# A banded attention with a gated mixture layer on one core: a new hand-over order of all engines' steps, with new bank and engine choices and re-measured costs in its planner

## The chip, the cores and the metric

The kernel runs on one core of one Trainium2 chip. The time is the device time of one execution in microseconds (us). Before the change three executions took 366.51, 365.14 and 366.31 us, so the median is 366.31 us. Nothing runs on the other cores.

## The reference

For 8 batches and 8 heads there are 512 local and 32 global positions of 64 numbers each. Local queries see the global keys and the local keys at most 32 positions away; global queries see every key. The 8 heads of a position together make a row of 512 numbers, and the 576 rows of a batch go through a gated layer: a causal convolution of five taps per channel makes the gate.

```python
k_all = np.concatenate([k_g, k_l], axis=2)
v_all = np.concatenate([v_g, v_l], axis=2)
s_g = scale * np.matmul(q_g, k_all.transpose(0, 1, 3, 2))
out_g = np.matmul(sm(s_g), v_all)
mask = np.abs(pos[:, None] - pos[None, :]) <= window
s_ll = np.where(mask, s_ll, -1000000000.0)
s_l = np.concatenate([s_lg, s_ll], axis=-1)
a_l = sm(s_l)
out_l = np.matmul(a_l, np.concatenate([v_g, v_l], axis=2))
...
gate = 1.0 / (1.0 + np.exp(-gate_pre))
val = x @ w_val
return (gate * val @ w_out).astype(np.float32)
```

## The kernel before, in words

The work is cut into 32 units (a pair of heads of one batch, numbered u), four to a batch b. Every step of a unit or a batch is a named task, and the string `ORDER` lists all 1,425 of them; each engine executes its own tasks strictly in that order, so the list is the schedule. A name can carry the engine after a colon (`xc13:DVE`) and, after an @, the PSUM bank or banks (there are 8) that the task's product is written to.

The tasks, with the lines of the profile:

- `iq`, `iv`, `wi` issue the loads of a unit's q and k (624 KB), of its v (975 KB) and of a weight (512 KB) on SP's queue (L405). The function `transfer` ties each such load to the last TensorE instruction that stands ahead of it in the list: SP waits for that one, so a load's place in the list is a time on TensorE.
- `s` are a unit's local scores (L552: 32 small products, a tiling of 64 rows by 32 columns of the array), `gs` a batch's global scores (L482, the same tiling). `mx` adds the mask and takes the row maxima on VectorE (L564), `exp` runs on ScalarE (L571), `t` transposes the result (L577), `tc` copies it out of PSUM, `av` multiplies by v (L588, a tiling of 128 by 32). `gmax`, `gexp`, `gt`, `gtc` and `gav` (L520) do the same for the global queries.
- `norm` divides (L598), `xt` transposes (L604), `xc` copies out. `xh` and `xl` split x in a high and a low half, `tap` and `conv` are the convolution (L640), `sig` the sigmoid. For the first two units the convolution runs as `pc` on TensorE (L665).
- `g1.b.e.t` are three 128x128x512 products each with w_val (L689), 16 such tasks a batch; `gv` multiplies by the gate, `gh` and `gl` split the result again, `g2.b.r.e` are three such products with w_out (L711), `ob` copies out, `st` stores. The group called g does the global rows at the end.
- `w0` to `w7` with `.s0` to `.s7` and `.high` turn a weight's 64-bit floats into two halves, on VectorE and ScalarE.

On TensorE there are therefore groups of many short instructions (an `s` is 64 weight loads and 64 multiplies by the profile's count) between long wide products (a `g1` part is three and three). TensorE's instructions come from memory over a DMA queue of their own (q8 in the profile).

The class `Plan` holds the tasks. Its method `order` walks `ORDER`, works out when each task would start by costs and lags written as numbers, and checks the bank of each; the list itself was found outside by annealing against those costs. At run time the numbers have one effect only: where the plan sees a gap on TensorE near the start, `keep_clock` puts in idle 128x512 products (L775) that fill it. In `order`, TensorE's instructions are counted in units (`FETCH`), and every 256 instructions a new packet of them has to be there; `BLOCK`, `STALL` and `AHEAD` say that it is asked for 72 instructions ahead of the packet's bound and needed 192 behind it, and `IDLE`, `BEGINS`, `LANDS`, `BUSY` how long it takes beside a load. `SWITCH` is the price of a change of tiling on TensorE between the classes of `MODE`.

Of the kernel before, what the change touches and what calls it, by code (L numbers as in the profile page):

```python
# [19 lines left out]
KW = 5  # L20
# [42 lines left out]
xc4 sig0 iq9 norm5 gv.0.0 w7.s0:ACT sig1 w7.s1 w6.s0:ACT w6.s1 s7@27 iq10 gv.0.1 sig2 g1.0.2.0@4 sig3 g1.0.2.1 g1.0.2.2
gt1.1@0 mx7.0 mx7.1 g1.0.2.3 g1.0.3.0@5 w7.s2 gtc1.1 gh.0.0 exp7.1 gl.0.0 gav1.1 exp7.0 w6.s2 gh.0.1 g1.0.3.1 av6@2
xt5@7 t7.1@0 tc7.1 w7.s3 w6.s3 w7.s4 w6.s4 g1.0.3.2 t7.0@1 g1.0.3.3 iv9 norm6 w6.s5 xh4 w7.s5 w6.s6 tc7.0 gv.0.2
g2.0.0.0@0 w6.high av7@2 xt6@4 w6.s7 gl.0.1 xc5 w7.high iq11 gh.0.2 w7.s6 gv.0.3 g2.0.0.1 gl.0.2 iv10 s8@71 w7.s7 gh.0.3
gl.0.3 norm7 g2.0.0.2 g2.0.0.3 g2.0.1.0@5 g2.0.1.1 g2.0.1.2 s9@23 mx8.0 ob.0.0 gnorm1 iv8 mx8.1 xl4 mx9.0 exp8.0 st.0.0
gs2@06 exp8.1 gx1@2 mx9.1 g2.0.1.3 gxc1 xh5 tap5 g2.0.2.0@3 ob.0.1 gmax2.0 t8.1@2 halo4:ACT t8.0@5 iq12 g2.0.2.1
tap4:ACT tc8.1 st.0.1 gexp2.0 conv4.0 g2.0.2.2 conv4.1 iv11 halo5:ACT xt7@2 tc8.0 conv4.2 gmax2.1 g2.0.2.3 xl5 iq13
av8@0 exp9.1 t9.1@5 ob.0.2 gexp2.1 norm8 g2.0.3.0@3 conv5.0 g2.0.3.1 gt2.0@0 exp9.0 conv4.3 conv5.1 st.0.2 xc7 xh7  # L70
conv5.2 tap7 tc9.1 g2.0.3.2 s10@67 t9.0@2 xl7 conv5.3 tc9.0 gtc2.0 g2.0.3.3 xt8@5 mx10.0 mx10.1 halo7:ACT exp10.0 xc6
iq14 g1.1.0.0@2 av9@0 conv7.0 xh6 gav2.0@7 s11@46 ob.0.3 norm9 conv7.1 g1.1.0.1 gt2.1@0 xl6 t10.0@3 mx11.0 mx11.1
conv7.2 halo6:ACT exp10.1 tap6:ACT t10.1@4 g1.1.0.2 conv6.0 gtc2.1 g1.1.0.3 tc10.1 xt9@4 conv7.3 conv6.1 exp11.1
g1.1.1.0@6 gav2.1 conv6.2 tc10.0 xc8:DVE av10@0 conv6.3 iq15 g1.1.1.1 norm10 iv12 g1.1.1.2 g1.1.1.3 sig4 sig5 xc9
tap9:ACT iv14 gv.1.0 g1.1.2.0@0 tap8 g1.1.2.1 gh.1.0:DVE g1.1.2.2 gnorm2 iv13 xh8 gv.1.1 g1.1.2.3 gx2@1 s12@67 gs3@42
gl.1.0 sig6 gh.1.1:DVE sig7 gv.1.2 gl.1.1 gh.1.2 xl8 g1.1.3.0@0 gmax3.0 g1.1.3.1 gxc2 exp11.0 mx12.0 mx12.1 g1.1.3.2
t11.1@1 g1.1.3.3 gmax3.1 gl.1.2 gv.1.3 halo9:ACT t11.0@7 gexp3.0 exp12.0 g2.1.0.0@6 tc11.1 tc11.0 halo8 gt3.0@4
gh.1.3:DVE gtc3.0 conv8.0 conv8.1 iq16 xt10@0 t12.0@7 exp12.1 gl.1.3 xh9 conv8.2 g2.1.0.1 conv8.3 xl9 xc10 g2.1.0.2
gexp3.1 av11@4 st.0.3 tc12.0 t12.1@1 g2.1.0.3 norm11 halo10:ACT xh10:DVE iv15 conv9.0 conv9.1 ob.1.0 tc12.1 g2.1.1.0@0
xl10 g2.1.1.1 s13@74 av12@2 mx13.0 xt11@1 g2.1.1.2 conv9.2 mx13.1 tap10 g2.1.1.3 g2.1.2.0@4 exp13.0 conv9.3 t13.0@5  # L80
g2.1.2.1 exp13.1 xc11 iq17 t13.1@1 conv10.0 norm12 conv10.1 xh11 s14@76 g2.1.2.2 g2.1.2.3 mx14.0 tc13.1 conv10.2 exp14.0
tc13.0 mx14.1 ob.1.2 st.1.0 conv10.3 xt12@1 xc12 av13@2 gav3.0@4 tap11 s15@56 norm13 halo11:ACT t14.0@1 exp14.1 xl11
mx15.0 xh12 iq18 t14.1@7 conv11.0 conv11.1 tc14.1 st.1.2 gt3.1@2 g2.1.3.0@5 gtc3.1 g2.1.3.1 iq19 gav3.1 ob.1.1:DVE xl12
tc14.0 av14@0 xt13@7 gnorm3 gx3@4 exp15.0 g2.1.3.2 iv16 g2.1.3.3 mx15.1 exp15.1 st.1.1 gxc3:DVE g1.2.0.0@4 conv11.2
conv11.3 norm14 xc13:DVE t15.0@6 sig8 t15.1@2 g1.2.0.1 iv17 tc15.1:DVE sig9 s16@70 iv18 mx16.0 mx16.1 xh13 g1.2.0.2
ob.1.3:DVE tap12:ACT halo12 g1.2.0.3 conv12.0 gv.2.0 conv12.1 tc15.0 xt14@7 conv12.2 g1.2.1.0@6 sig10 conv12.3 sig11
g1.2.1.1 g1.2.1.2 exp16.1 xc14 g1.2.1.3 av15@4 gh.2.0 tap14:ACT gv.2.1 norm15 gs4@02 iv19 halo14 gl.2.0 s17@76 iq20
mx17.0 halo13 t16.1@4 gmax4.0 exp17.0 gmax4.1 xl13 gh.2.1 gexp4.0 g1.2.2.0@5 g1.2.2.1 tc16.1 xt15@7 g1.2.2.2 g1.2.2.3
gl.2.1 gexp4.1 g1.2.3.0@0 g1.2.3.1 exp16.0 gv.2.2 xh14:DVE mx17.1 tap13 gt4.0@4 t16.0@1 g1.2.3.2 t17.0@6 g1.2.3.3 gtc4.0
tc17.0 gav4.0@4 conv13.0 exp17.1 gt4.1@2 xl14 conv13.1 gtc4.1 gh.2.2 gv.2.3 tc16.0 gh.2.3 st.1.3 g2.2.0.0@6 t17.1@5  # L90
conv13.2 conv14.0 conv13.3 g2.2.0.1 gav4.1 tc17.1:DVE xc15 iq21 av17@0 av16@2 gl.2.3 gnorm4 xh15 gl.2.2 halo15:ACT
g2.2.0.2 norm16 iv21 g2.2.0.3 xt16@7 g2.2.1.0@2 tap15 g2.2.1.1 g2.2.1.2 g2.2.1.3 ob.2.0 g2.2.2.0@6 s18@34 xl15 conv15.0
norm17 s19@50 ob.2.1 conv14.1 st.2.1 g2.2.2.1 xt17@2 conv14.2 mx18.0 mx18.1 iv20 g2.2.2.2 mx19.0 mx19.1 conv14.3
g2.2.2.3 g2.2.3.0@3 st.2.0 exp18.1 g2.2.3.1 t18.1@0 exp19.0 gx4@1 exp19.1 iq22 conv15.1 g2.2.3.2 g2.2.3.3 xc17 conv15.2
xh17:DVE t19.1@2 gxc4 tc19.1:DVE g1.3.0.0@1 exp18.0 conv15.3 t18.0@5 g1.3.0.1 t19.0@2 g1.3.0.2 xl17 tap17 halo17 xc16
g1.3.0.3 conv17.0 ob.2.3 tc18.0 iq23 tc19.0:DVE tc18.1 av18@4 conv17.1 ob.2.2 sig12 norm18 av19@6 conv17.2 g1.3.1.0@0
sig13 tap16 xt18@4 g1.3.1.1 gv.3.0 g1.3.1.2 sig14 norm19 xh16 halo16 gh.3.0 g1.3.1.3 iv22 s20@15 gs5@62 conv17.3 gv.3.1
xc18 mx20.0 mx20.1 exp20.1 iv23 tap18 xl16 s21@40 g1.3.2.0@5 gl.3.0 gh.3.1 g1.3.2.1 gmax5.0 g1.3.2.2 st.2.2 mx21.0
exp20.0 halo18 t20.1@1 mx21.1 g1.3.2.3 t20.0@4 conv16.0 gv.3.2 gexp5.0 gh.3.2:DVE gl.3.1 sig15 gmax5.1 xt19@6 tc20.0
tc20.1 st.2.3 g1.3.3.0@7 conv16.1 iq24 gexp5.1 g1.3.3.1 conv16.2 g1.3.3.2 conv16.3 g1.3.3.3 gt5.0@0 g2.3.0.0@4 g2.3.0.1  # L100
av20@2 gtc5.0 xc19 gav5.0@5 xh18 s22@60 gv.3.3 gh.3.3:DVE gl.3.2 norm20 exp21.0 t21.0@7 xh19 exp21.1 g2.3.0.2 tap19:ACT
gl.3.3 g2.3.0.3 halo19:ACT xl19 xl18 mx22.0 g2.3.1.0@1 g2.3.1.1 tc21.0:DVE conv18.0 conv18.1 exp22.0 mx22.1 ob.3.0
gt5.1@2 g2.3.1.2 t21.1@4 iq25 tc21.1:DVE t22.0@7 gtc5.1 conv18.2 g2.3.1.3 xt20@0 gav5.1 conv18.3 av21@2 exp22.1 xc20
iq26 g2.3.2.0@4 conv19.0 gnorm5 t22.1@0 gx5@5 g2.3.2.1 ob.3.1 conv19.1 g2.3.2.2 xh20:DVE s23@16 conv19.2 tc22.1 st.3.1
# [895 lines left out]
```

## Time and profile before

| what | value |
|---|---|
| median of 3 executions | 366.31 us (365.14 to 366.51) |
| the profiled execution | 369.17 us, of which the span from first to last instruction is 367.4 us |
| busy, TensorE multiplies / weight loads | 353.4 us / 278.8 us |
| busy, VectorE / ScalarE | 322.7 us / 243.8 us |
| granted TensorE clock, mean | 0.995 |
| HBM read / written | 56.87 MB / 8.91 MB |

The span is the time between the first and the last instruction; the other 1.8 us of the profiled execution lie around it. PE is TensorE, PEld its weight loads, DVE VectorE, ACT ScalarE, SP the engine whose queue issues loads; a `q` behind a name is that engine's sequencer. In the timeline a row has its start, its length and the instruction with xcount; what stands in brackets is idle time just before it and what ended that. "issue" is idle time for which the profile shows nothing that was waited for. Multiplies overlap in the array, so a row's length is not the time it costs: the distance between two starts is.

### The profile page before, as it was taken

The numbers are of one execution on the slowest core, as the hardware profiler recorded it, in microseconds if no ns is written. First come the engines' busy times: TensorE is split into PE (matmuls) and PEld (weight loads), VectorE is DVE, ScalarE is ACT, GpSimd is POOL, SyncE is SP. The second block draws the span as 40 slices with busy tenths as digits, with TensorE's granted clock in tenths as the row PEclk, the third lists the DMA queues.
The fourth block names the chain that finished last, engine by engine and source line by source line (L and its number), as shares of the span: only waits on it lengthen the run. The fifth ranks groups of instructions, "written<-read, shape, count | busy, mean of one in ns | idle before, by whom it ended". The sixth has DMA issues, their size and how long they took to land.

```text
span 367.4 us, 14722 instructions
## 1 busy us (share of the span) xinstructions
PE 353.4 (96%) x6334; PEld 278.8 (76%) x6334; DVE 322.7 (88%) x1079; ACT 243.8 (66%) x566; POOL 0.8 (0%) x7
## 2 busy tenths in 40 slices
PE   7799999999999999999997999999999999999995
PEld 3556668778788788787886888788877888888894
DVE  4999999999999998998797899999889876997972
ACT  4898799867978689673787858777775456333030
POOL 0000000000000000000000000000000000000000
PEclk9999999999999999999998999999999999999999
DMA  8996896389276459816555155570775101010223
GB/s 291 396 347 200 281 378 249 108 318 307 79 228 248 152 157 320 309 60 215 180 191 168 63 196 184 190 269 4 243 244 221 61 2 59 30 58 2 86 86 86
DMA packets 17248, 66.72 MB, mean 182 GB/s; under 512 B 1952, under 2 KB 4000, under 8 KB 17184
## 3 DMA queue, kind: packets, MB, share of 16 engines
q1 hardware_dynamic: 12240, 57.12, 44.5%
q10 hardware_dynamic: 4944, 8.67, 6.5%
q8 instruction: 49, 0.80, 0.9%
q14 instruction: 15, 0.12, 0.1%
HBM read 56.87 MB, written 8.91 MB: 179 GB/s over the span
## 4 chain that ended last, share of the span: by engine, by line
PE 78%; DVE 12%; DMA 6%; issue 2%; ACT 1%; SPq 1%; DVEq 0%; ACTq 0%
PE psum L711 24%; PE psum L689 23%; PE psum L588 7%; PE psum L552 7%; PE psum L577 7%; PE psum L604 3%; DMA v<-in_vw_dram 3%; DVE pm L564 3%; PE psum L520 2%; DMA wraw<-in_w_out_dram 2%; DVE gate L640 1%; PE psum L500 1%; PE psum L482 1%; DMA qk<-in_qk_dram 1%; DVE xs L598 1%
## 5 line engine op out<-in xcount | busy, mean ns | idle before, releaser
L571 ACT ACTIVATE pm<-pm,mx 128x128 f32<-128x128 f32 x256 | 80.8, 393 | 22.7 <-DVE mx L564 22.4
L640 DVE SCALAR_TENSOR_TENSOR gate<-xc,cw,gate 128x512 f32<-128x512 f32 x120 | 87.7, 747 | 1.6 <-ACT gate L386 0.4
L564 DVE CUSTOM_DVE_ANT_0 pm<-psum,mask 128x128 f32<-128x128 f32 x256 | 57.3, 286 | 3.8 <-PE psum L552 3.7
L689 PE MATMUL psum<-xh,wvh 128*128 128x512 f32 x128 | 54.9, 429 | 0.1
L711 PE MATMUL psum<-woh,gh 128*128 128x512 f32 x128 | 54.7, 428 | 0.0
L689 PE MATMUL psum<-xl,wvh 128*128 128x512 f32 x128 | 51.0, 398 | 2.0 <-issue 2.0
L689 PE MATMUL psum<-xh,wvl 128*128 128x512 f32 x128 | 50.7, 396 | 0.0
L711 PE MATMUL psum<-woh,gl 128*128 128x512 f32 x128 | 50.4, 394 | 0.0
L711 PE MATMUL psum<-wol,gh 128*128 128x512 f32 x128 | 50.1, 391 | 0.0
L577 PE MATMUL psum<-ident,pm 128*128 128x128 f32 x256 | 39.8, 281 | 1.1 <-ACT pm L571 1.0
L552 PE MATMUL psum<-qk 64*32 64x128 f32 x2048 | 37.0, 273 | 2.3 <-issue 1.4
L577 PEld LDWEIGHTS psum<-ident,pm 128*128 128x128 f32 x256 | 30.8, 142 | 10.9 <-ACT pm L571 3.1
L588 PEld LDWEIGHTS psum<-v,pts 128*32 128x32 f32 x2048 | 30.5, 109 | 9.9 <-issue 4.1
L552 PEld LDWEIGHTS psum<-qk 64*32 64x32 f32 x2048 | 29.0, 105 | 11.2 <-issue 5.5
L588 PE MATMUL psum<-v,pts 128*32 128x65 f32 x2048 | 34.7, 221 | 1.5 <-DMA v<-in_vw_dram 1.3
L393 ACT COPY pts<-psum 128x512 f32<-128x512 f32 x50 | 28.3, 584 | 7.3 <-PE psum L577 7.1
L393 ACT COPY ob<-psum 128x512 f32<-128x512 f32 x27 | 15.7, 585 | 23.4 <-PE psum L711 20.2
L393 ACT COPY xc<-psum 128x512 f32<-128x512 f32 x27 | 15.7, 582 | 21.9 <-DVE gate L640 11.2
L697 DVE TENSOR_TENSOR gv<-psum,gate 128x512 f32<-128x512 f32 x32 | 21.9, 685 | 9.5 <-PE psum L689 9.3
L689 PEld LDWEIGHTS psum<-xh,wvh 128*128 128x128 f32 x128 | 24.4, 190 | 5.9 <-issue 1.3
L689 PEld LDWEIGHTS psum<-xl,wvh 128*128 128x128 f32 x128 | 24.3, 190 | 5.8 <-issue 2.5
L711 PEld LDWEIGHTS psum<-woh,gl 128*128 128x128 f32 x128 | 24.0, 188 | 5.7 <-DVE gl L703 0.4
(109 smaller groups left out, 559.7 us busy)
## 6 DMA issues: line engine op xcount, KB each, us to landing
v<-in_vw_dram SPq DMA_DIRECT2D x32, 975.0 KB, 7.2
qk<-in_qk_dram SPq DMA_DIRECT2D x32, 624.0 KB, 4.7
out_dram<-ob ACTq DMA_DIRECT2D x32, 256.0 KB, 2.2
wraw<-in_w_val_dram SPq DMA_DIRECT2D x4, 512.0 KB, 12.2
wraw<-in_w_out_dram SPq DMA_DIRECT2D x4, 512.0 KB, 4.7
mask<-in_mask_dram SPq DMA_DIRECT2D x1, 256.0 KB, 4.5
out_dram<-obg SPq DMA_DIRECT2D x4, 64.0 KB, 1.7
out_dram<-obg ACTq DMA_DIRECT2D x4, 64.0 KB, 2.0
```

The source lines that it names most:

```text
L393: A.copy(out, in_)
L520: on_pe(T.matmul(ag[SG * c:SG * c + SG, :], pgt[:k, s, SG * c:SG * c + SG], vt[:k, w, h, :], start=(n == 0), stop=(n == len(steps) - 1)))
L552: on_pe(T.matmul((sx, sy)[h][32 * j:32 * j + 32, i, :], qkt[rows, 32 * m:32 * m + 32], qkt[rows, k0:k0 + P], start=True, stop=True))
L564: V.tensor_tensor_reduce(out=pm[:, h, i, :], in0=s[:, i, :], in1=mask[:, i, :], op0=ALU.add, op1=ALU.min, scale=-SCALE, scalar=3.0e38, acc ...
L571: A.activation(out=pm[:, h, i, :], in_=pm[:, h, i, :], func=AF.Exp, bias=mx[:, c:c + 1], scale=-1.0)
L577: on_pe(T.transpose(pt[:, i, :], pm[:, h, i, :], ident))
L588: on_pe(T.matmul(ax[32 * j:32 * j + 32, h, E1 * i:E1 * i + E1], pts[:, h, i, 32 * j:32 * j + 32], vt[:, block_win(4 * i + j), h, :], start ...
L604: on_pe(T.transpose(xt[:, P * i:P * i + P], xs[:, i].rearrange("p h d -> p (h d)"), ident))
L640: V.scalar_tensor_tensor(out=acc, in0=xc[:, k:k + SL], scalar=cw[:, u % NDT, k:k + 1], in1=acc, op0=ALU.mult, op1=ALU.add)
L689: on_pe(T.matmul(box["pv", e], w[:, e, t * P:t * P + P], x, start=(t == 0 and q == 0), stop=(t == NDT - 1 and q == 2)))
L697: V.tensor_tensor(out=box["gv", e], in0=box["pv", e], in1=gates[x0 + e], op=ALU.mult)
L711: on_pe(T.matmul(box["po", r], g[:, e, rs], w[:, e, :], start=(e == 0 and q == 0), stop=(e == NDT - 1 and q == 2)))
```

## The change

`ORDER` is replaced as a whole: the same 1,425 tasks in another order, with other banks, and with another engine for 94 of them (VectorE's instructions go from 1,041 to 1,047 rows, ScalarE's table loads from 18 to 20). The planner's numbers are new, its model of an instruction fetch lets a fetch wait to the end of any load under way when it is sent, without a limit, and a fetch takes DMA time itself; transposes become a tiling class of their own.

```diff
-sig13 tap16 xt18@4 g1.3.1.1 gv.3.0 g1.3.1.2 sig14 norm19 xh16 halo16 gh.3.0 g1.3.1.3 iv22 s20@15 gs5@62 conv17.3 gv.3.1
-xc18 mx20.0 mx20.1 exp20.1 iv23 tap18 xl16 s21@40 g1.3.2.0@5 gl.3.0 gh.3.1 g1.3.2.1 gmax5.0 g1.3.2.2 st.2.2 mx21.0
+g1.3.1.2 sig15 xh18 g1.3.1.3 st.2.2 gv.3.1 av19@2 norm19 s20@51 mx20.0 s21@04 st.2.3 mx21.0 gs5@26 mx20.1 g1.3.2.0@5
+iv21 iv23 exp20.0 g1.3.2.1 exp21.0 g1.3.2.2 mx21.1 gmax5.0 iq24 g1.3.2.3 conv17.0 gmax5.1 g1.3.3.0@4 gh.3.1 gl.3.1
...
-IDLE, BEGINS, LANDS, BUSY = 3050, 1400, 1200, 2600
-MODE = {"s": 0, "gs": 0, "av": 1, "gav": 1}
-SWITCH = ((0, 185, 185), (130, 0, 110), (110, 90, 0))
+IDLE, BEGINS, LANDS, SPREAD, TAKES = 3050, 150, 800, 0, 900
+MODE = {"s": 0, "gs": 0, "av": 1, "gav": 1, "t": 2, "xt": 2, "gt": 2, "gx": 2}
+SWITCH = ((0, 190, 190, 295), (112, 0, 113, 192), (94, 93, 0, 0), (92, 93, 0, 0))
...
-                now = MODE.get(kind(t.name), 2)
+                now = MODE.get(kind(t.name), 3)
...
-                        wait = [b - sent for a, b in self.loads if a <= sent < b]
-                        here = sent + IDLE + min([BUSY, max(wait, default=0)])
+                        wait = [b - sent for a, b in self.loads if a - SPREAD <= sent < b + SPREAD]
+                        here = sent + IDLE + max(wait + [0])
+                        if free["DMA"] > sent:
+                            free["DMA"] += TAKES
...
-        plan.add(f"gs{b}", "PE", 1050, lambda b=b: g_s(b), [f"lq{u}" for u in units] + ([f"gs{b - 1}"] if b else []),
+        plan.add(f"gs{b}", "PE", 916, lambda b=b: g_s(b), [f"lq{u}" for u in units] + ([f"gs{b - 1}"] if b else []),
```

The other costs change in the same way (an `av` from 1040 to 933, a `g2` from 700 to 682, a `t` from 380 to 436, and so on); no instruction's own operands change.

On TensorE, around unit 16's scores (rows named qk, 32 short products) in batch 2 the list had, before, transposes, a wide product, the scores, and wide products again:

```order
L577 MATMUL psum<-ident,pm_2490 128x128 x8
L689 MATMUL psum<-xh_2135,wvh 128x512
L689 MATMUL psum<-xl_2136,wvh 128x512
L689 MATMUL psum<-xh_2135,wvl 128x512
L552 MATMUL psum<-qk_2120 32x128 x32
L689 MATMUL psum<-xh_2197,wvh 128x512
L689 MATMUL psum<-xl_2198,wvh 128x512
```

In the changed kernel, whose line numbers are 5 higher, there stand at unit 16's scores:

```order
L716 MATMUL psum<-woh,gl_1966 128x512
L593 MATMUL psum<-v_2153,pts_2317 32x65 x32
L593 MATMUL psum<-v_2249,pts_2470 32x65 x32
L557 MATMUL psum<-qk_2340 32x128 x32
L609 MATMUL psum<-ident,xs_2663 128x128 x4
L694 MATMUL psum<-xh_2027,wvh 128x512
L694 MATMUL psum<-xl_2028,wvh 128x512
```

The two products with v of units 14 and 15 now stand right ahead of the scores, and the transposes of unit 14 between the scores and the next wide product. Over the whole list, short groups (`s`, `gs`, `av`, `gav`) that a wide product (`g1`, `g2`, `pc`) follows directly go from 24 to 8, and short groups that follow a wide product or a transpose from 47 to 43.

On TensorE around unit 21's scores in batch 3, before, the end of the global scores of batch 5 (the last of 16 such rows), the scores and the products of task `g1.3.2.0`:

```order
L482 MATMUL psum<-qk_3313 32x160
L552 MATMUL psum<-qk_3009 32x128 x32
L689 MATMUL psum<-xh_2511,wvh 128x512
L689 MATMUL psum<-xl_2512,wvh 128x512
L689 MATMUL psum<-xh_2511,wvl 128x512
```

In the changed kernel the scores of units 20 and 21 stand together, behind the products with v of unit 19 and ahead of the global scores:

```order
L694 MATMUL psum<-xh_3100,wvl 128x512
L593 MATMUL psum<-v_2772,pts_3241 32x65 x32
L557 MATMUL psum<-qk_2921 32x128 x32
L557 MATMUL psum<-qk_3034 32x128 x32
L487 MATMUL psum<-qk_2921 32x384
L487 MATMUL psum<-qk_3034 32x384
```

The loads of v that the list had ahead of unit 20's and unit 21's scores (`iv22`, `iv23` in the diff) have moved: `iv22` far ahead, into batch 2, and `iv23` behind the whole of the short groups and one task of wide products.

More of the change, by code (lines that the diff above doesn't have):

```diff
@@ L71 @@
[L71 to L80, printed above, removed]
@@ new lines @@
+g2.0.2.0@4 conv4.0 g2.0.2.1 conv5.2 t9.0@5 conv4.1 st.0.0 iv11 tc8.1 conv4.2 exp9.1 tc9.0 g2.0.2.2 g2.0.2.3 gs2@26
+t9.1@5 ob.0.2 g2.0.3.0@4 st.0.1 iv10 conv4.3 conv5.3 gmax2.0 tc8.0 xt7@0 g2.0.3.1 xc6 g2.0.3.2 gmax2.1 xc7 g2.0.3.3
+av8@0 xh6 ob.0.3:DVE xl6 xh7 tc9.1 av9@4 iq12 iq13 halo7 gexp2.0 s10@23 st.0.3 halo6 gexp2.1 tap6:ACT norm8 xt8@0
+g1.1.0.0@1 xl7 mx10.0 gt2.0@6 tap7:ACT gtc2.0 norm9 conv7.0 g1.1.0.1 mx10.1 s11@67 conv7.1 exp10.0 exp10.1 gav2.0@4
+t10.0@5 conv6.0 mx11.0 iq14 conv6.1 conv7.2 iq15 exp11.0 tc10.0 g1.1.0.2 g1.1.0.3 mx11.1 gt2.1@2 conv6.2 conv7.3 gtc2.1
@@ L291, in put @@
                     self.rings[name][2][key] = t.end + LAG[t.eng]
-            if t.eng == "DMA":
-                self.loads = self.loads[-11:] + [(t.start + BEGINS, t.end + LANDS)]
+            if t.eng == "DMA" and t.name != "first":
+                self.loads = self.loads[-15:] + [(max([t.start + BEGINS] + [b for _, b in self.loads[-1:]]), t.end + LANDS)]
             line.append(t)
@@ L444, in weight @@
         wraws[k] = load
-        for n, ns in enumerate(((("DVE", 320), ("ACT", 520)), (("DVE", 320), ("DVE", 320)), 360, 560, 320, 540, 320, 540)):
+        for n, ns in enumerate(((("DVE", 338), ("ACT", 585)), (("DVE", 336), ("DVE", 336)), 336, 602, 336, 602, 336, 602)):
             plan.add(f"w{k}.s{n}", *((ns, 0) if n < 2 else ("DVE", ns)), lambda n=n: step(n),
@@ L853, in attention_moe @@
+        plan.add(f"xh{u}", (("ACT", 515), ("DVE", 335)), 0, lambda u=u: l_xh(u), [f"xc{u}"], take=[("xh", u), ("xl", u)], lock=True)
         plan.add(f"xl{u}", (("DVE", 600), ("DVE", 600)), 0, lambda u=u: l_xl(u), [f"xh{u}"], lock=True)
@@ L872, in attention_moe @@
         plan.add(f"fv{u}", "FREE", 0, lambda: None, [f"av{u}", f"gav{b}.0", f"gav{b}.1"], give=[("v", u)])
-    plan.add("cw", "DVE", 1300, taps, ["craw"], take=[("mx", "cv")], give=[("mx", "cv")])
+    plan.add("cw", "DVE", 1410, taps, ["craw"], take=[("mx", "cv")], give=[("mx", "cv")])
     plan.given("start", 0.0)
```

248 lines of the change are left out of this document (128 added, 120 removed).

## The prediction

> **What bounds the kernel now.** I read the page first, then TensorE's timeline, then windows and SP's queue.
>
> ```profile
> PE 353.4 (96%) x6334; PEld 278.8 (76%) x6334; DVE 322.7 (88%) x1079; ACT 243.8 (66%) x566; POOL 0.8 (0%) x7
> ...
> q8 instruction: 49, 0.80, 0.9%
> ...
> PE 78%; DVE 12%; DMA 6%; issue 2%; ACT 1%; SPq 1%; DVEq 0%; ACTq 0%
> ```
>
> TensorE is busy in 96% of the span and holds 78% of the chain that ended last. The change alters none of its products, so the time can only come from four things: the start, changes of tiling, waits, and the end. The start first, a row of TensorE's timeline:
>
> ```profile
> 14.27 1.11 PE L588 MATMUL psum<-v,pts 128*32 128x65 f32 x64 [1.34 <-DMA v<-in_vw_dram]
> ```
>
> and the windows from 5 to 80 us (length, then busy time by engine; the row "sum" adds all four):
>
> ```profile
> 5.00:20.00 15.00, 12.29 (x317) 7.64 (x316) 13.57 (x73) 11.54 (x35) 0.00 (x0) 1.00 1.05 400
> 60.00:80.00 20.00, 19.75 (x396) 15.12 (x396) 19.62 (x79) 15.17 (x35) 0.00 (x0) 1.00 0.60 214
> sum 75.00, PE 70.15 PEld 49.34 DVE 71.69 ACT 62.02 POOL 0.00; mean PE 17.54 PEld 12.33 DVE 17.92 ACT 15.50 POOL 0.00
> ```
>
> The first product with v waits for its load until 14.27 us, and from 5 to 80 us VectorE is busy 71.69 of 75 us: it, not TensorE, sets when the first `g2` can run. Behind 80 us TensorE waits seldom, and where it does the releaser is "issue". These are the largest such places:
>
> ```profile
> 93.49 0.29 PE L520 MATMUL psum<-v,pgt 96*32 96x65 f32 x6
> 94.18 0.73 PE L520 MATMUL psum<-v,pgt 96*32 96x65 f32 x34 [0.40 <-issue]
> 94.84 1.16 PE L552 MATMUL psum<-qk 64*32 64x128 f32 x64
> 95.92 0.50 PE L689 MATMUL psum<-xh,wvh 128*128 128x512 f32 x1
> 96.26 0.39 PE L689 MATMUL psum<-xl,wvh 128*128 128x512 f32 x1
> 96.48 0.39 PE L689 MATMUL psum<-xh,wvl 128*128 128x512 f32 x1
> ...
> 170.53 1.80 PE L552 MATMUL psum<-qk 64*32 64x128 f32 x110
> 172.54 0.59 PE L552 MATMUL psum<-qk 64*32 64x128 f32 x18 [0.22 <-issue]
> 173.07 0.50 PE L711 MATMUL psum<-woh,gh 128*128 128x512 f32 x1
> ...
> 193.13 0.40 PE L689 MATMUL psum<-xh,wvh 128*128 128x512 f32 x1
> 195.56 0.50 PE L689 MATMUL psum<-xl,wvh 128*128 128x512 f32 x1 [2.02 <-issue]
> ...
> 266.16 0.86 PE L552 MATMUL psum<-qk 64*32 64x128 f32 x39
> 267.59 1.53 PE L552 MATMUL psum<-qk 64*32 64x128 f32 x89 [0.57 <-issue]
> 269.05 0.50 PE L711 MATMUL psum<-woh,gh 128*128 128x512 f32 x1
> ```
>
> At 193 us nothing is shown that the product waits for, and VectorE and ScalarE had fed it long before. TensorE ran out of instructions: 6334 multiplies and 6334 weight loads in 49 packets (q8, 0.80 MB) are 259 instructions a packet, a `g1` part uses six of them in 0.7 us, an `s` 128 in 0.9 us. Short groups in a row eat a packet in about 2 us. What was on the DMA engines then, by SP's timeline and by the windows (behind the engines' columns stand the granted clock, the DMA engines' busy share and GB/s):
>
> ```profile
> 188.66 2.38 SPq L405 DMA_DIRECT2D v<-in_vw_dram  x2
> ```
>
> ```profile
> 193.40:195.60 2.20, 0.17 (x2) 0.04 (x1) 2.17 (x18) 2.10 (x5) 0.00 (x0) 1.00 0.93 314
> 195.60:200.00 4.40, 4.40 (x19) 3.83 (x20) 2.49 (x7) 1.99 (x4) 0.00 (x0) 0.61 0.22 83
> ```
>
> Two loads of v, issued at 188.66 and within 2.4 us, kept the DMA engines 93% busy while TensorE stood still, and behind the stall the granted clock was 0.61 for 4.40 us. That costs 0.39 x 4.40 = 1.7 us more, together with 2.02 us of idle time 3.7 us.
>
> [...]
>
> **The change part by part.** *Instruction fetches.* I count instructions along both lists, with the two numbers that the planner holds (asked for 72 ahead of a packet's bound, needed 192 behind it), and lay the trace's durations beside them. Fetches with under 5 us of TensorE work between the two points: 16 before, 15 after, so the lists are equally dense. What differs is the loads. Among those 16, seven have a load placed in the 2 us before the fetch is asked for (near the scores of units 4, 6, 14, 18, 20, 23 and 28); three of the four costly places above are among them. Among the 15 of the new list none has. So I let those stalls go. Behind each, a group is longer than its own work. The global product took 94.84 - 93.49 = 1.35 us where others take 0.71, by a row of the chain and two of the timeline:
>
> ```profile
> 100.82 0.71 PE psum L520 x40
> ```
>
> ```profile
> 188.56 1.16 PE L552 MATMUL psum<-qk 64*32 64x128 f32 x63
> 189.46 0.48 PE L482 MATMUL psum<-qk 64*32 64x384 f32 x1
> ```
>
> That is 0.64. One `s` takes 189.46 - 188.56 = 0.90 us, and 95.92 - 94.84 = 1.08 when a wide product follows: two in a row 1.98. At 170.53 they took 2.54 (0.56 over), at 266.16 2.89 (0.91 over). With the 3.7 the four come to 5.8 us, and without the long one to 2.1. New stalls: three dense fetches have a load 3 to 4 us ahead (a weight near unit 4's product, v of unit 10 near unit 9's product, q of units 14 and 15 near `gav2.1`), which is nearest to the place at 93 us, where one of the loads stood 4.5 us ahead. At 0.64 each that is 1.9; the first lies where VectorE is behind anyhow and costs nothing, so 1.3. It could be 0 (no stall without a load close ahead), or 3.7 at each of two (7.4).
>
> *Tilings.* A short group followed by a wide product: 24 before, 8 after. The rows at 94.84 price it: the scores take 1.08 in place of 0.90, and the first wide product 96.26 - 95.92 = 0.34 in place of 0.22. With a transpose between, by the timeline and, for eight transposes, by the chain:
>
> ```profile
> 22.95 1.16 PE L552 MATMUL psum<-qk 64*32 64x128 f32 x64
> 24.04 0.66 PE L577 MATMUL psum<-ident,pm 128*128 128x128 f32 x4
> ...
> 91.34 0.60 PE L604 MATMUL psum<-ident,xs 128*128 128x128 f32 x4
> 91.69 0.47 PE L689 MATMUL psum<-xh,wvh 128*128 128x512 f32 x1
> 92.00 0.40 PE L689 MATMUL psum<-xl,wvh 128*128 128x512 f32 x1
> 92.24 0.39 PE L689 MATMUL psum<-xh,wvl 128*128 128x512 f32 x1
> 92.56 1.11 PE L588 MATMUL psum<-v,pts 128*32 128x65 f32 x64
> ```
>
> ```profile
> 238.99 0.87 PE psum L577 x8
> ```
>
> The scores take 1.09, just as much; four transposes ahead of a wide product take 91.69 - 91.34 = 0.35 in place of 0.87 / 2 = 0.435, and the first product takes 0.31. So the transposes give 0.085 back where the wide product loses 0.09 to 0.12, but they would do so elsewhere as well. The gain lies between 0 and 0.12 a place; I take half, 0.06, and 16 x 0.06 = 1.0. Short groups entered from the wide products or transposes go from 47 to 43; the last wide product ahead of a short group takes 92.56 - 92.24 = 0.32 in place of 0.22, so an entry costs 0.1, and four make 0.4. Together 1.4 us, between 0.4 and 2.3.
>
> [...]
>
> *The start.* `t1.1` now stands ahead of the first product with v, so 0.44 us of transposes run while TensorE waits for that load. But the path to the first `g2` goes through VectorE: 111 of its tasks stand ahead of it up to `gl.0.3` before, 110 after, and the TensorE work beside them is the same to 0.7 us. So the start can gain only what VectorE idles, 75 - 71.69 = 3.3 us at the very most, nearly all of it short gaps between steps. I take 0.4, between -1 (VectorE waits more) and 1.5.
>
> *Engines and end.* The two more table loads cost ScalarE
>
> ```profile
> L673 ACT ACT_TABLE_LOAD x9 | 11.5, 1283 | 0.2
> L717 ACT COPY obg<-psum 128x256 f32<-128x256 f32 x1 | 0.4, 372 | 5.9 <-PE psum L711 5.9
> ```
>
> 2 x 1.283 = 2.6 us; it is busy 66% and waits 5.9 us for TensorE at the very end, so that hides. Were the cover gone, 2.6 us would show. The last stores are the same instructions in both, and cost nothing.
>
> *The sum.* On the profiled execution: 369.17 - 5.8 + 1.3 - 1.4 - 0.4 = 362.9. The median of 366.31 is 2.86 us below that execution, less than the 3.7 of the long stall. If the timed runs lack this stall, its gain is not theirs: 366.31 - 2.1 + 1.3 - 1.4 - 0.4 = 363.7. If they have it, 360.0. They spread over 1.4 us, and the lowest, 365.14, is near 369.17 - 3.7 = 365.5, so the first is likelier; I take **363.0**.
>
> **The rivals.** (1) *Fetches do not wait for loads.* Then where a load stands is worth nothing, the dense stretches stall as often as before (15 against 16), and only tilings and start remain: 366.31 - 1.4 - 0.4 = 364.5. For it: of the seven fetches with a load close ahead, those near units 14 and 23 have no row of waiting for "issue" in the timeline. Against it: the 0.93 DMA share in the long stall. [...]
>
> (2) *The new pairs of loads meet the fetch* (slower). The list issues q of units 12 and 13 in one go behind `av9`, where the fetch for units 10 and 11 is asked for, and q of 14 and 15 in one go ahead of `gav2.1`. A pair of loads is what stood ahead of the stall of 2.02 us. If both places stall with a slowed clock, 363.0 + 2 x 3.7 = 370.4; one alone gives 366.7, no change. It turns slower once the two together pass 5.1 us. For it: a pair in one go was costly. Against it: a pair of q is 1,248 KB, of v 1,950 KB:
>
> ```profile
> v<-in_vw_dram SPq DMA_DIRECT2D x32, 975.0 KB, 7.2
> qk<-in_qk_dram SPq DMA_DIRECT2D x32, 624.0 KB, 4.7
> ```
>
> (3) *The timed runs have the long stall too,* and it goes: 360.0. The change not doing what it says is no rival: the order shows it moved.
>
> **How the numbers follow.** My forecast has 0.52, rival 1 0.20, rival 2 0.17 (0.12 for both places, 0.05 for one), rival 3 0.08, and 0.03 is for a start that loses its 1 us. About 0.5% (1.83 us) is what a measurement of this kernel can tell from no change: faster means under 364.48, slower over 368.14. Rival 1 lies on the edge and is halved. Faster: 0.52 + 0.08 + 0.10 = 0.70. Same: 0.10 + 0.05 + 0.03 = 0.18. Slower: 0.12. The range goes from rival 3, 360.0, to 367.0, which holds one bad place and leaves out both.
>
> **What would show it.** Right: no "issue" row over 1 us on TensorE behind 80 us, a granted clock of 1.00 in every window, the sum of such rows behind 80 us near 1 us in place of 3.2; the first `g2` at about the same time after the same TensorE work; VectorE still at 95% to 80 us. Wrong: an "issue" row of 2 us behind `av9` or `gav2.1` with a clock under 1; TensorE waiting for VectorE or ScalarE behind 80 us, which I priced at nothing; or dense groups stalling with no load near, which would be rival 1.

## The result, and the profile after

The changed kernel takes 363.28 us (median of 9 runs), the kernel before 367.22 us beside it: 0.9895 of the time, 95% interval 0.9861 to 0.9930. Two further sets of runs, on other occasions, give 0.9898 (0.9864 to 0.9933) and 0.9884 (0.9842 to 0.9927) for the same kernel. So it is faster by about 1.1%, 0.3 us from the forecast.

The first profiled execution of the changed kernel ran at a mean granted clock of 0.559 and is not read here; the profile below is of a later execution of the same kernel, 363.40 us with a span of 361.6 us. (A correction to the text before: a batch has 544 rows, not 576.)

From its page, TensorE's share, the fetch queue and the chain:

```profile
PE 351.3 (97%) x6333; PEld 278.1 (77%) x6333; DVE 322.1 (89%) x1079; ACT 248.5 (69%) x568; POOL 0.9 (0%) x7
...
q8 instruction: 49, 0.80, 0.9%
...
PE 74%; DVE 16%; DMA 6%; ACT 2%; issue 1%; ACTq 0%; DVEq 0%
```

The work and the 49 packets of instructions are the same. What TensorE waits for behind 60 us (total, times, longest):

```profile
PE psum L557 <- ACT ob L398: 0.9, 1, 0.9
PE psum L593 <- DVE ob L400: 0.7, 1, 0.7
PE psum L716 <- ACT ob L398: 0.3, 1, 0.3
```

These are all its rows. Before, "issue" rows summed to 3.2 us there; now there is none. In their place stand three waits for a copy out of a bank (`ob`). They differ between executions: 1.9 us here, one wait of 1.25 us (at 88 us) in another profile of the same kernel, and 0.2 us in that of the kernel with four loads put back (below). ScalarE's timeline at two of them:

```profile
84.30 0.59 ACT L398 COPY ob<-psum 128x512 f32<-128x512 f32 x1 [1.79 <-DMA out_dram<-ob]
...
226.79 0.59 ACT L398 COPY ob<-psum 128x512 f32<-128x512 f32 x1 [1.23 <-DMA out_dram<-ob]
```

There are two `ob` buffers. The copy waits until the store of the last but one has landed, the bank stays taken, and TensorE stands still behind it: 0.3 us at 84.93, and 0.95 at 227.43 ahead of unit 25's scores. The place of the old long stall, units 20 and 21 on TensorE's timeline, and the first 80 us by windows:

```profile
187.17 2.03 PE L557 MATMUL psum<-qk 64*32 64x128 f32 x128
188.94 1.18 PE L487 MATMUL psum<-qk 64*32 64x384 f32 x32
190.05 0.50 PE L694 MATMUL psum<-xh,wvh 128*128 128x512 f32 x1
```

```profile
5.00:20.00 15.00, 13.05 (x314) 8.09 (x313) 12.96 (x70) 11.39 (x33) 0.00 (x0) 1.00 1.04 398
...
60.00:80.00 20.00, 19.89 (x410) 15.53 (x409) 19.66 (x82) 17.76 (x43) 0.00 (x0) 1.00 0.60 197
sum 75.00, PE 72.22 PEld 51.64 DVE 71.74 ACT 66.23 POOL 0.00; mean PE 18.06 PEld 12.91 DVE 17.94 ACT 16.56 POOL 0.00
```

The two scores take 188.94 - 187.17 = 1.77 us, nothing but their own work. VectorE is busy 71.74 of 75 us, as before (71.69).

Where the time went is read at two points that have the same TensorE work ahead of them in both lists: the second task of the first `g2` group and the first `g2` of the last group. Before:

```profile
71.65 0.48 PE L711 MATMUL psum<-woh,gh 128*128 128x512 f32 x1
```

and after:

```profile
70.92 0.48 PE L716 MATMUL psum<-woh,gh 128*128 128x512 f32 x1
...
351.84 0.39 PE L716 MATMUL psum<-woh,ghg 128*128 128x512 f32 x1
```

The second point was reached at 357.63 us before. So 71.65 - 70.92 = 0.73 us were won up to the first point, and (357.63 - 71.65) - (351.84 - 70.92) = 5.06 us between the two. The four places of the prediction (93, 173, 193 and 269 us) can be priced by the kernel of the first experiment, which has the same TensorE list and no "issue" row at these places. The same rows took 1.35 us before against 0.68 there, 2.54 against 1.96, 7.09 (from 193.13 to 200.22 us, with the slow clock) against 3.25, and 2.89 against 1.96: 0.67, 0.58, 3.84 and 0.93 us more, 6.0 in all. In the changed kernel no "issue" row is left at these groups. The new waits are 1.9 us; before, TensorE waited 0.4 us for other engines there. That leaves 5.06 - 6.0 + 1.9 - 0.4 = 0.6 us, a remainder, for the tilings and all else.

### The profile page after: what moved, and what is told of

Same layout as the page of the kernel before. It is cut to its first block, busy times and chain, and to the rows that moved or that the text cites. A ratio compares the mean times of both kernels' runs of the same rounds, so it can differ in the third digit from the quotient of the medians.

```text
span 568.4 us, 14715 instructions
## 1 busy us (share of the span) xinstructions
PE 562.5 (99%) x6333; PEld 361.2 (64%) x6333; DVE 328.4 (58%) x1079; ACT 250.8 (44%) x568; POOL 0.9 (0%) x7
## 4 chain that ended last, share of the span: by engine, by line
PE 98%; DVE 1%; ACT 1%; issue 0%
PE psum L694 28%; PE psum L716 28%; PE psum L593 9%; PE psum L557 9%; PE psum L582 8%; PE psum L609 4%; PE psum L525 3%; PE psum L670 3%; PE psum L487 2%; PE psum L505 2%; PE psum L507 1%; PE psum L780 1%; ACT pm L576 0%; PE psum L538 0%; DVE pm L569 0%; DVE wa L367 0%
## 5 line engine op out<-in xcount | busy, mean ns | idle before, releaser
L716 PE MATMUL psum<-woh,gh 128*128 128x512 f32 x128 | 78.9, 617 | 0.0
L694 PE MATMUL psum<-xh,wvh 128*128 128x512 f32 x128 | 78.0, 610 | 0.0
L694 PE MATMUL psum<-xh,wvl 128*128 128x512 f32 x128 | 74.0, 578 | 0.0
L694 PE MATMUL psum<-xl,wvh 128*128 128x512 f32 x128 | 73.9, 577 | 0.0
L716 PE MATMUL psum<-wol,gh 128*128 128x512 f32 x128 | 73.9, 577 | 0.0
L716 PE MATMUL psum<-woh,gl 128*128 128x512 f32 x128 | 73.5, 574 | 0.0
L582 PE MATMUL psum<-ident,pm 128*128 128x128 f32 x256 | 59.2, 374 | 0.1
L593 PE MATMUL psum<-v,pts 128*32 128x65 f32 x2048 | 54.3, 285 | 0.3 <-DVE wraw L374 0.3
L694 PEld LDWEIGHTS psum<-xh,wvl 128*128 128x128 f32 x128 | 27.9, 218 | 20.4 <-issue 11.5
L716 PEld LDWEIGHTS psum<-woh,gh 128*128 128x128 f32 x128 | 28.4, 222 | 16.1 <-issue 8.2
```

Source lines behind the costliest of these rows:

```text
L582: on_pe(T.transpose(pt[:, i, :], pm[:, h, i, :], ident))
L593: on_pe(T.matmul(ax[32 * j:32 * j + 32, h, E1 * i:E1 * i + E1], pts[:, h, i, 32 * j:32 * j + 32], vt[:, block_win(4 * i + j), h, :], start ...
L694: on_pe(T.matmul(box["pv", e], w[:, e, t * P:t * P + P], x, start=(t == 0 and q == 0), stop=(t == NDT - 1 and q == 2)))
L716: on_pe(T.matmul(box["po", r], g[:, e, rs], w[:, e, :], start=(e == 0 and q == 0), stop=(e == NDT - 1 and q == 2)))
```

## The experiments

### The loads alone, in the kernel before

Six loads moved in the kernel before (the expectation says seven and names six); the instructions of all other engines stand in the same order.

```diff
-gh.3.0 g1.3.1.3 iv22 s20@15 gs5@62 conv17.3
-mx20.0 mx20.1 exp20.1 iv23 tap18 xl16 s21@40 g1.3.2.0@5
+gh.3.0 g1.3.1.3 s20@15 gs5@62 conv17.3
+mx20.0 mx20.1 exp20.1 tap18 xl16 s21@40 g1.3.2.0@5 iv22 iv23
...
+s19@50 iv21
+s29@64 iq30 iv28 iq31
```

> The kernel before with only seven loads' places changed (v of units 21, 22, 23, 28 and q of 30, 31, moved from ahead of a dense stretch of short TensorE groups to right behind it); TensorE, VectorE and ScalarE run the same list. Theory: the waits for "issue" at 170, 193 and 266 us go: 1.5 us faster than the kernel before if its timed runs lack the long stall, up to 5.2 us if they have it; the profile has no such row at those places. Rival (fetches do not wait for loads): no change, and the rows stay.

Measured: 365.96 us beside 366.47, ratio 0.9970 (0.9941 to 1.0000): a gain of 0.5 us at the edge of what the runs can tell, where the theory had at least 1.5. TensorE's timeline at the global product that had stalled at 93 us, at the old long stall, and a row further on:

```profile
94.05 0.76 PE L520 MATMUL psum<-v,pgt 96*32 96x65 f32 x40
94.73 1.16 PE L552 MATMUL psum<-qk 64*32 64x128 f32 x64
...
188.18 1.16 PE L552 MATMUL psum<-qk 64*32 64x128 f32 x64
189.07 1.18 PE L482 MATMUL psum<-qk 64*32 64x384 f32 x32
189.99 1.13 PE L552 MATMUL psum<-qk 64*32 64x128 f32 x64
191.22 0.50 PE L689 MATMUL psum<-xh,wvh 128*128 128x512 f32 x1
...
272.24 1.13 PE L482 MATMUL psum<-qk 64*32 64x384 f32 x26 [0.54 <-DMA qk<-in_qk_dram]
```

The stalls at 173, 193 and 269 us are gone. So is the one at 93 us (0.40 us of waiting before, none here), though no load near it was moved: a short stall also comes and goes from one execution to the next, and one profile without it proves little.

The trace also records when each packet of q8 begins; I count TensorE's instructions from j x 256 for packet j, with the planner's 256; 12,668 instructions in 49 packets are 259 each. The packet that TensorE ran out for began at 193.16 us before, when TensorE had started 449 instructions from that point; here it began at 189.66 us, at 283. That is 3.5 us earlier, and 3.1 us earlier when counted from the same instruction of TensorE (1.3 us behind the 152nd in place of 4.4). It is one execution against one.

The edit also has a cost of its own: q of unit 31, moved back, came late, and the global scores took 273.30 - 270.86 = 2.44 us up to the next wide product, where they took 1.08 before (277.01 - 275.93). That is 1.36 us, of which 0.54 is the wait shown.

It also matters how often the long stall happens. Of 67 runs of the kernel before, 13 had a mean clock of 0.995 or less, as the profiled execution had; their median is 369.13 us, that of the other 54 is 366.53. With the loads moved, 1 of 12 had such a clock. So the long stall strikes at most about one run in five: a slow clock at another place lowers the mean as much (to 0.994 in the changed kernel's execution with a low clock at its start, below), and that each of the 13 runs had the stall was not shown. It also means that most executions lack it with the loads where they were.

### The loads put back, in the changed kernel

The changed kernel once more beside it, and one with five loads of v put back right ahead of dense stretches.

```diff
+gv.3.1 av19@2 iv21 iv23 norm19 s20@51
+tc23.0:DVE iv27 iv25 av23@2
+tc28.1 iv30 av28@0 norm28 gav7.0@4
```

> The changed kernel once more, for a profile at full clock. Theory (loads moved away from instruction fetches, fewer changes of tiling): 363.3 us timed; on TensorE no row of waiting for "issue" over 1 us behind 80 us, such rows 1 us in all behind 80 us where the kernel before had 3.2, granted clock 1.00 in every window, first g2 after as much time as before. Rival (fetches do not wait for loads): as many such rows as before, 3 us in all.

> The changed kernel with only five loads moved back to right ahead of dense stretches (v of 21 and 23 ahead of the scores of 20 and 21, v of 27 and 25 ahead of the product with v of 23, v of 30 ahead of that of 28). Theory: a stall at each, 0.6 to 2 us, with a slowed clock behind the long ones: 1.5 to 9 us slower than the changed kernel, most likely 4, so near 367. Rival (fetches do not wait for loads): 363.3, no change.

Measured: the changed kernel 363.17 us, ratio 0.9898. Its profile has no "issue" row behind 80 us, as expected, but not a clock of 1.00 in every window: it was low from 14.75 to 18.16 us (see the end). With the loads back it took 369.63 us, ratio 1.0087 (1.0055 to 1.0119). That looks like a proof, and its timeline and windows show that it is none:

```profile
286.04 1.19 PE L525 MATMUL psum<-v,pgt 96*32 96x65 f32 x34 [4.32 <-DMA v<-in_vw_dram]
```

```profile
286.00:300.00 14.00, 13.96 (x309) 11.93 (x310) 6.99 (x35) 3.91 (x8) 0.00 (x0) 0.88 0.02 4
```

`gav7.0` needs v of unit 30, whose load the edit had issued only 5 us earlier. It waited 4.32 us for data, and the clock of 0.88 over 14 us cost more. So four of the five were tried again without that one:

> The changed kernel with four loads of v (units 21 and 23 ahead of the scores of unit 20; 27 and 25 ahead of av23) back ahead of dense stretches. The earlier run also moved the load of unit 30 to just ahead of av28, and in its trace gav7.0 then waited 4.3 us for data; this one leaves that load alone. Theory (a load just ahead of a dense stretch holds the fetch): 364.7 to 367, with TensorE waiting 0.6 to 2.5 us near the scores of unit 20 or near av23. Second theory (nearly all of the 6.5 us of the earlier run was that wait for data and the slower clock behind it): 363.0 to 364.3.

Measured: 362.05 us, ratio 0.9885 (0.9846 to 0.9925); the first theory's forecast of 364.7 to 367 failed. Its TensorE timeline at units 20 and 21:

```profile
186.02 2.03 PE L557 MATMUL psum<-qk 64*32 64x128 f32 x128
187.79 1.18 PE L487 MATMUL psum<-qk 64*32 64x384 f32 x32
188.89 0.50 PE L694 MATMUL psum<-xh,wvh 128*128 128x512 f32 x1
```

No stall. The packet of q8 began at 187.19 us, 0.1 us behind the first bytes of the load: it went out with the load, not behind it, took 2.25 us in place of about 0.95, and was in time. A load ahead of a dense stretch in the list is therefore not enough. In this execution the load was not on the queue ahead of the fetch; that this decides is tested next.

### The fetch beside loads, alone

TensorE with nothing but wide products and two scores per period; the rest of the computation is left out.

```python
for phase, n in ((0, 0), (1, 1), (2, 2)):
    for k in range(10):
        wide(12)
        for m in range(n):
            load(4 + (2 * k + m) % 28)
        s_group()
        s_group()
        wide(12)
```

> TensorE alone, everything else of the computation left out: 10 periods of 24 wide products, 2 groups of scores (128 short products) and no load, then 10 with one load of v issued just ahead of the scores, then 10 with two. Theory (an instruction fetch ends no earlier than the loads in flight): the periods of the first part are alike to 0.1 us; of the second and third parts those in which a fetch falls behind a load are longer by 0.5 to 3.5 us, more with two loads than with one. Rival 1 (a fetch takes its turn with the loads): all three parts have the same period to 0.3 us.

Measured, by the timeline, without a load and with two:

```profile
29.08 2.03 PE L941 MATMUL psum<-qk 64*32 64x128 f32 x128
...
36.75 2.03 PE L941 MATMUL psum<-qk 64*32 64x128 f32 x128
...
182.41 2.03 PE L941 MATMUL psum<-qk 64*32 64x128 f32 x128
...
190.08 2.03 PE L941 MATMUL psum<-qk 64*32 64x128 f32 x128
```

All periods are 7.67 us long, so by the periods the rival wins. The records of q8 say otherwise. From the moment at which TensorE starts its 152nd instruction behind j x 256, a point taken for the count alone, to the start of packet j it takes 1.05 us in the median without loads, 2.9 with one load a period and 3.8 with two. So the fetches did wait for loads; these stretches of 256 short instructions only left them enough time. Laid beside the records of the loads, the wait is plain: in the part with one load, 9 of the 11 packets began in the last 0.5 us of a load (loads from 106.79 to 110.30, 114.46 to 117.75 and 122.13 to 125.76 us; packets at 109.83, 117.43 and 125.76 us, and so on). One began 0.1 us behind a load's first bytes and was not put off, as in the run above; one met no load. A fetch did not wait for everything on the queue, though: in the kernel before, the two loads moved from 189.62 to 197.49 us, and the packet began at 193.16.

### Longer dense stretches beside loads

The same with three scores in a row (five in the last part) between 28 wide products.

```diff
-        for phase, n in ((0, 0), (1, 1), (2, 2)):
+        for n, groups in ((0, 3), (1, 3), (2, 3), (0, 5)):
```

> TensorE alone again, all else of the computation left out: 7 periods each of 28 wide products with 3 groups of scores (192 short products in a row) and no load, the same with one load of v just ahead of the scores, the same with two, and with 5 groups (320 in a row) and no load. Theory (a fetch begins about 1 us after TensorE passes the 152nd instruction ahead of it when no load runs, 3 to 4 us after it when loads run, and TensorE runs out some 300 instructions later, which are 2.4 us of scores): no stall over 1 us without a load with 3 groups; with a load one to three of the seven periods stall by 1 to 3.5 us; with 5 groups and no load some stall by 0.3 to 1 us. Rival 1 (loads make no difference): the second and third parts stall as the first does, to 0.3 us.

Measured, from the timeline (rows with waits; the four parts begin near 29, 99, 175 and 251 us):

```profile
42.19 0.87 PE L941 MATMUL psum<-qk 64*32 64x128 f32 x41 [1.24 <-issue]
...
125.14 0.65 PE L941 MATMUL psum<-qk 64*32 64x128 f32 x9 [4.14 <-issue]
...
170.70 2.22 PE L946 MATMUL psum<-xr 128*128 128x512 f32 x7 [1.91 <-issue]
...
202.21 0.44 PE L941 MATMUL psum<-qk 64*32 64x128 f32 x13 [3.38 <-issue]
...
247.52 3.98 PE L946 MATMUL psum<-xr 128*128 128x512 f32 x11 [3.45 <-issue]
...
341.56 0.27 PE L941 MATMUL psum<-qk 64*32 64x128 f32 x1 [1.73 <-issue]
```

Without a load three of seven periods stall by 0.8 to 1.24 us. With one load three stall, by 0.8, 1.9 and 4.1, with two three again, by 1.0, 3.4 and 3.5. So rival 1 fails, and the theory was wrong in part: it allowed no stall over 1 us without a load. Five scores in a row without any load stall in every period, by 1.0 to 1.7 us each time. So there are two parts: dense stretches of 384 instructions (three scores) stalled by 0.8 to 1.24 us by themselves, where those of 256 in the bench before did not; and in two of the three stalls of each part with loads the wait is 0.7 to 2.9 us longer than the longest without.

The records of q8 fit the first part. In all the profiles read here no two packets begin less than 3.27 us apart, and 256 instructions of scores take 1.8 us (2 x 0.90). They also tie the stalls to the fetch: each of their 28 "issue" waits on TensorE ends 2.2 to 2.6 us behind the start of a packet.

### The same in the changed kernel

Two loads of v issued later, the last near 88 us in place of 86, closer to the dense stretch at 90 us.

```diff
-t9.0@5 conv4.1 st.0.0 iv11 tc8.1
-ob.0.2 g2.0.3.0@4 st.0.1 iv10 conv4.3
+tc8.0 xt7@0 g2.0.3.1 iv11 iv10 xc6
```

> The changed kernel with two loads of v (units 11 and 10) moved from beside the stores of row blocks 0 and 1 of batch 0 to behind g2.0.3.1. Theory (the loads of units 9, 11 and 10 run without a gap from 76 to 91 us, the stores of row blocks 0 and 1 land among them, and ob.0.2 with the bank it frees waits for the first store): the store lands 2 us earlier, the wait for ScalarE at 85 us is under 0.2 us, that for VectorE's ob at 90 us under 0.3, and the time is 0.5 to 1.3 under the changed kernel's 362.9, that is 361.6 to 362.4. Rival (the later loads hold the fetch that goes out in av9 or the data of unit 10): an issue row of 1 to 3 us between 90 and 100 us, 363.5 to 366.

Measured: 364.12 us (363.09 to 366.42), ratio 0.9937 (0.9909 to 0.9965), 1.2 us over the changed kernel's 362.90 in the set of runs before it. Its timeline, and its window of the stall:

```profile
93.76 0.40 PE L694 MATMUL psum<-xh,wvl 128*128 128x512 f32 x1
94.08 0.42 PE L557 MATMUL psum<-qk 64*32 64x128 f32 x6
95.81 1.11 PE L557 MATMUL psum<-qk 64*32 64x128 f32 x58 [1.31 <-issue]
```

```profile
94.50:95.80 1.30, 0.00 (x1) 0.00 (x0) 1.30 (x9) 1.30 (x6) 0.00 (x0) 1.00 1.04 420
```

The rival came: TensorE ran out of instructions for 1.31 us while loads filled the DMA engines. The packet began at 93.38 us, 434 instructions from j x 256; in the changed kernel's profile it began at 92.01, at 404, and TensorE did not wait. The theory fell too, for the copy `ob.0.2` still waited 1.94 us for the store, so these two loads do not hold it.

### The new waits and the start

Two stores issued earlier on ScalarE; three more products that nothing reads ahead of `av0`; and the first of these together with the four loads, beside the changed kernel.

```diff
+ob.0.0 st.0.0 conv5.0
+t9.1@5 st.0.1 ob.0.2 g2.0.3.0@4
```

> The changed kernel with two stores of the output of batch 0 issued earlier on ScalarE: row block 0 right behind its copy, row block 1 ahead of the copy of row block 2. Theory (g2.0.3.0 waits 1.25 us for a bank since ob.0.2 waits 2.73 us for the store of row block 0): the wait at 88 us goes to under 0.3 us and the time falls by 0.6 to 1.3, to 361.9 to 362.6. Rival (VectorE bounds this place, the wait covers for a later one): 363.0 to 363.4, with a wait for VectorE of about 1 us behind 88 us.

Measured: 362.56 us (361.55 to 363.71), ratio 0.9883 (0.9850 to 0.9916); the wait at 85 us is 0.47 us in its profile, not gone. The time lies in the theory's range; whether by the edit, the combination below decides.

```diff
                 if not opened and gap > KEEP:
                     keep_clock(int((gap - 400) * 0.55 / 235), t.spare)
+                if t.name == "av0":
+                    keep_clock(3, t.spare)
```

> The changed kernel with three more products that nothing reads ahead of av0. Theory (the profile of the changed kernel had the granted clock at 0.5 from 15 to 18 us since TensorE idled between 12.9 and 14.3 us, and many timed runs with a mean clock of 0.995 to 0.998 had the same): the clock is 1.00 in the first 30 us, the mean clock of most runs is 0.999 or more, and the time falls by 0.3 to 1.0, to 362.2 to 362.9. Rival (VectorE sets the pace up to 80 us and hides it): 363.0 to 363.4 at the better clock.

Measured: 363.21 us (362.79 to 365.26), ratio 0.9907 (0.9875 to 0.9939). The rival came: TensorE's early clock changes nothing that the end feels beyond what a run can tell. Its clock is 1.00 over the first 40 us, but so it was in the changed kernel's other profile. The windows of the execution that raised the question, that of the changed kernel run beside the five loads:

```profile
14.00:16.00 2.00, 1.74 (x77) 1.59 (x84) 1.20 (x4) 1.26 (x3) 0.00 (x0) 0.69 1.13 416
16.00:18.00 2.00, 2.00 (x72) 1.69 (x64) 1.18 (x4) 0.67 (x1) 0.00 (x0) 0.50 0.97 377
```

> The changed kernel with both edits of the two kernels that measured lowest: the four loads ahead of the dense stretches and the two stores issued earlier. Theory (the wait for the bank falls from 1.2 to about 0.5 us and the loads change nothing, since their fetches go out just ahead of them): 0.3 to 1.0 under the changed kernel run beside it. Rival (both differences were chance): within 0.3 of it.

> The changed kernel itself, beside the combination: 362.5 to 364.0, with the wait of 1.1 to 1.3 us for the bank that ob.0.2 frees, near 86 us, and no issue row over 0.5 us behind 80 us.

Measured: 363.00 us together, 362.90 for the changed kernel beside it. In the combination's profile the wait at 86 us is 1.26 us, as in the changed kernel's other profile (1.25); in that of the changed kernel beside it, where 1.1 to 1.3 was expected, it is 0.32. So the rival holds: the differences of the single edits were within chance, and no version here is shown to beat the changed kernel.

### The tilings alone

TensorE only: 20 periods in which the scores go straight to a wide product, then 20 in which four transposes stand between; all else is left out.

> Leaves out the whole computation; TensorE alone runs 20 periods of scores, 6 wide products, 4 transposes, 6 wide products, then 20 periods of scores, 4 transposes, 12 wide products, with no loads. The difference of the two periods is what a direct exit from the scores into a wide product costs. My term: 0.06 us a period (0 to 0.12). The planner's numbers of the changed kernel: 0.105. If each change of tiling costs the same whatever follows: 0.

Measured, from the timeline:

```profile
31.33 1.16 PE L941 MATMUL psum<-qk 64*32 64x128 f32 x64
32.42 1.66 PE L946 MATMUL psum<-xr 128*128 128x512 f32 x6
...
35.84 1.16 PE L941 MATMUL psum<-qk 64*32 64x128 f32 x64
...
143.59 1.16 PE L941 MATMUL psum<-qk 64*32 64x128 f32 x64
144.67 0.66 PE L950 MATMUL psum<-ident,qk 128*128 128x128 f32 x4
...
148.03 1.16 PE L941 MATMUL psum<-qk 64*32 64x128 f32 x64
```

The period is 35.84 - 31.33 = 4.51 us in the one order and 148.03 - 143.59 = 4.44 in the other: 0.07 us a place, for scores; no other short group was tried. The scores themselves take 1.09 and 1.08, whatever follows.

## Why the prediction was right, and where it was not

- **The four stalls go.** Right in the profiles: 6.0 us against the 5.8 forecast, and 2.2 against 2.1 without the long one. That fetches wait for loads is shown by the bench: a packet of q8 begins 1.05 us after its point without loads, 2.9 to 3.8 beside them, and with one load mostly just as it ends. In the two kernels it rests on one execution each: a fetch 3.1 us earlier with the loads moved away, and a stall of 1.31 us with loads moved near. Rival 1 is out.
- **The rule by which I counted was too coarse.** "A load in the 2 us before the fetch is asked for" neither is enough (the four loads put back cost nothing) nor is needed (dense stretches can stall by about 1 us alone). It also marks two of the four costly places by its own terms, not three: the fetch near 170 us had more than 5 us of room (TensorE took 6.2 us between the two points) and was not on the list of 16. As far as these runs show, what decides is whether the load is on the queue ahead of the fetch (9 of 11 packets of the bench began in the last 0.5 us of a load; two packets, one there and one with four loads put back, that began 0.1 us behind a load's first bytes were not put off), and a list does not show that.
- **New stalls, +1.3.** The size was right by luck and the mechanism wrong. Behind 80 us no fetch stalls in the changed kernel's two profiles. The loss, 1.5 us net in the one read above, comes from copies that wait for stores, and so banks that come free late. The prediction named TensorE waiting for ScalarE or VectorE behind 80 us, and priced it at nothing: this is the step that failed. I had not followed the two `ob` buffers through the new order.
- **Tilings, -1.4.** The bench gives 16 x 0.07 = 1.1 where 1.0 was taken, if all short groups behave as scores do; the four entries at 0.1 were not measured. The profile leaves 0.6 as a remainder behind 71 us, so the 1.4 is not confirmed as a whole. Did each change of tiling cost the same whatever follows, the two periods would be equal; they differ by 0.07 us.
- **The start, -0.4.** 0.73 us were won up to the first point of equal work. How that splits is not shown: the kernel before also had a fifth "issue" wait, of 0.65 us at 50.6 us, which the prediction left out. VectorE (busy 71.74 of the 75 us) sets the pace there, as the prediction said, and the kernel with three more products (363.21 us) agrees.
- **Which execution counts.** The prediction chose between 363.7 (timed runs without the long stall) and 360.0 (with it) and took 363.0. At most about one run in five has it, so the first was right for the median. By the rows of the two profiles the 54 other runs should gain 2.2 (the three short stalls) + 0.7 + 0.6 - 1.5 = 2.0 us, to 364.5; they gain 3.2 to 3.6. Some 1.2 to 1.6 us of the gain stay unexplained; the profiles are one execution each, and the new waits, 1.9 us in one and 0.2 in another, may be less in most runs, which is not shown. That the forecast came within 0.3 us is therefore in part luck.
- **Rival 2, pairs of loads meeting the fetch,** did not come: behind `av9` and at `gav2.1` the changed kernel has no "issue" row. The run with v's loads moved to shortly ahead of `av8` shows that a load near there can stall it, by 1.31 us rather than 3.7.

## What to carry to other kernels

Short instructions in long rows need their fetch in time: 384 of them in a row stalled by 0.8 to 1.24 us in three of seven periods without a load. And in these runs the fetch waited for a load that was on the queue ahead of it: its packet began 2.9 to 3.8 us after its point, where it took 1.05 without loads. Look for idle time that nothing explains behind a dense stretch, then read from the trace when the fetch's packet began, not only where the load stands in the list. When stalls are removed, follow the buffers of the stores as well: in the changed kernel a copy waited 1.23 us for a store to land and held a bank, and the bank held TensorE for 0.95 us.

## What the hardware showed that was not expected

The granted clock was low behind some idle times of TensorE, of 1.31 to 4.32 us, and 1.00 behind others, of 1.24 to 1.44 us. Windows of the dense bench right behind stalls of 1.24, 4.14 and 1.73 us, in this order:

```profile
42.20:46.00 3.80, 3.80 (x54) 3.11 (x54) 0.00 (x0) 0.00 (x0) 0.00 (x0) 1.00 0.02 4
...
125.10:129.00 3.90, 3.86 (x17) 2.80 (x17) 0.00 (x0) 0.00 (x0) 0.00 (x0) 0.50 0.02 4
...
341.60:345.00 3.40, 3.40 (x10) 2.58 (x10) 0.00 (x0) 0.00 (x0) 0.00 (x0) 0.63 0.00 0
```

Behind the stalls of 1.91, 3.38 and 3.45 us it was 0.63, 0.55 and 0.69; behind two of 1.44 us it was 1.00. The length of the stall alone did not decide. In the changed kernel's other profile an idle time of 1.31 us ahead of 14.26 us was followed by a low clock (0.50 from 14.75 us), and in the kernel before one of 1.34 us ahead of 14.27 us was not. The next windows are 3.41 us each: two at the long stall of the kernel before, cut where the clock changes, two at the changed kernel's start, cut the same way, and one at the start of the kernel before, where it did not change:

```profile
192.91:196.32 3.41, 1.39 (x7) 0.81 (x6) 3.38 (x21) 3.30 (x7) 0.00 (x0) 1.00 0.92 312
196.32:199.73 3.41, 3.41 (x16) 3.01 (x14) 1.50 (x4) 1.01 (x3) 0.00 (x0) 0.50 0.11 40
...
11.34:14.75 3.41, 2.10 (x40) 1.20 (x44) 3.27 (x7) 3.41 (x12) 0.00 (x0) 1.00 1.00 379
14.75:18.16 3.41, 3.41 (x124) 2.81 (x121) 1.86 (x7) 1.19 (x4) 0.00 (x0) 0.50 1.03 399
...
11.99:15.41 3.42, 2.08 (x76) 1.44 (x83) 3.06 (x13) 3.00 (x10) 0.00 (x0) 1.00 1.06 392
```

Each low stretch in the profiles read here, the last at a kernel's end apart, is at 0.50 and lasts 3.41 us (6.83 behind the stall of 4.14 us). Its start is not that of the stall: in the kernel before TensorE waited from 193.54 to 195.56 us, and the clock was low from 196.32. In the long stall's case TensorE had been busy for 1.39 of the 3.41 us ahead of it; at the two starts it was 2.10 and 2.08 us, and the clock dropped in the one and not in the other. So, by my estimate from these windows, a stall followed by one stretch of 3.41 us costs up to 0.50 x 3.41 = 1.7 us more than its own length, where TensorE sets the pace.
